# Raw weights behind the branch, units 4 to 7 placed before r*k, middle units gathered in float32

## The chip, the cores and the metric

One core of one Trainium2 chip runs the whole program as one launch. The time is device microseconds of that core, the median over several executions; the kernel before is at 474.01 us (472.36 to 475.83).

## The reference

Three layers follow one another: a linear recurrence with heads (2 batches, 8 heads, 768 steps, 48 wide), a mixture of 8 experts in which each token goes to one, and a gated MLP.

```python
for t in range(S):                      # recurrence, per batch and head
    cur = einsum('bhd,bhe->bhde', u * k_t, v_t)
    y[:, :, t] = einsum('bhd,bhde->bhe', r_t, state + cur)
    state = w_t[..., None] * state + einsum('bhd,bhe->bhde', k_t, v_t)
x = y as (N = 1536 tokens, D = 384)
logits = x @ w_gate; e = argmax(logits); gate = softmax(logits)[e]
# token i takes the next free slot of its expert (at most `capacity`, 384)
h = relu(x[slots of e] @ w1[e]); out = gate * (h @ w2[e])    # F = 1024
g = out @ w_gate2; result = (silu(g) * (out @ w_val)) @ w_out   # d_ff = 1536
```

## The kernel before

The tokens are cut into 12 units of 128 (u = 0 to 11), six per batch. For each unit the recurrence is done in chunk form: `scores` makes the masked matrix A on TensorE, ScalarE and GpSimd, `values` multiplies it with v and adds the carried state (`Sb`, written by `expand`), `own` and `xrow` add the token's own term, `r*k` (`prep3`, line 428) feeds `diag`, which gives that own term's factor. `gate_t` transposes x, `logits` (or `gate_rows` with `columns`) makes the gate's 8 logits.

Units are chosen in groups: 0 to 3, 4 to 7 ("four"), 8 and 9 ("two"), 10 and 11 ("last"). `choose` takes the maximum, the one-hot `ohs` and the softmax's weight on VectorE and ScalarE; `count` makes running counts on TensorE; `place` turns them into slots. `weigh` makes the weighted rows `xg` on ScalarE (line 593), and `scatter` writes them to `scr` in HBM by an indirect DMA from GpSimd (line 751), into the experts' slots.

Expert 0's input does not go through HBM for the last four units: `onehot` (line 806) compares a unit's slots with a row of column numbers, and `x0_add` (line 829) gathers x transposed, straight into PSUM, with the one-hot as the moving side. There x is split into a high and a low fp32r half: `x0_high` on ScalarE (line 815), `x0_low` on GpSimd for units 8 and 9 (line 821) and on VectorE for 10 and 11 (line 823). The units before come back from `scr` into `zrow` (`x0_load`) and are added with the identity, in float32. `parts` splits the result into `xe0`.

Weights are raw float32 tiles of 768 KB, loaded by SyncE's queue (`load_raws`, line 169) into three pools: `RAWS = 5, 2, 3` buffers, one of the first five being xe0's. ScalarE casts a piece to its high half (`high`, line 207) and VectorE subtracts for the low half (`low`, line 212). In the unit loop six are loaded; the last pool lies where the recurrence's tiles lay, so it opens behind `early.close()`. `st["held"]` stops further loads. When both halves of a raw tile are made, `low` calls for more loads.

Program order on each engine is what the text writes, except that short VectorE steps kept in `steps` are put in by `tick` and `flush`. `tc.mark_branch_hint_location` announces the branch `tc.If(most > SLOTS)`, into which the program would go if an expert had more than 240 tokens; all engines read a count and compare (line 1239). Behind it the experts run: `m1` (line 1300), `relu`, `m2` (line 1318), with `fill` and `need` putting in the weights' steps, then the MLP (lines 1413 and 1436). `warm` issues 512-column matmuls whose result is not used (line 452).

The tail of the attention, lines 948 to 1066, is written out by hand and is where nearly all of the change lies. Of the PSUM tiles there, the counts and logits of units 4 to 11 share one tile, `lgs`.

Of the kernel before, what the change touches and what calls it, by code (L numbers as in the profile page):

```python
# [26 lines left out]
NU = N // C  # L27
# [15 lines left out]
def build(tc, cap, dm, tk, vt, ub, cst, wg, w1, w2, wgate, wval, wout, out):  # L43
# [113 lines left out]
    def load_raws(upto):  # L157
        while not st["held"] and st["loaded"] < min(upto, len(raws_)):
            free_ = [p for p in rps if len(p[2]) < p[1] or p[2][-p[1]] in done]
            if not free_:  # L160
                return
            free_[0][2].append(st["loaded"])
            src = raws_[st["loaded"]]
            t = raw_t[st["loaded"]] = free_[0][0].tile([128, 1536], F32, tag="raw", name="raw")
            if len(src.shape) == 3 and src.dtype != F32:
                k = src.shape[1]
                nc.sync.dma_start(out=t.bitcast(I32).rearrange("p (k f) -> p k f", k=k), in_=src.bitcast(I32))
            else:
                nc.sync.dma_start(out=t.rearrange("p (k f) -> p k f", k=src.shape[1]), in_=src)
            st["loaded"] += 1  # L170
# [382 lines left out]
            nc.tensor.matmul(ps[32 * k:32 * k + 32], wgs[:, k, :], xgt[w][:, k, :], start=False, stop=True,  # L553
                             skip_group_check=True)

    lgs = []

    def logits_to(u):
        g = group[u]
        if g not in lgt:  # L560
            if g[-1] < NU - 5:
                lgt[g] = ps1.tile([128, len(g), 3 * E], F32, tag="lg", name="lg")
            else:
                i = g[0] % 4 + 4 * (g[0] > 7)
                if not i:
                    lgs.append(ps1.tile([128, 8, 3 * E], F32, tag="lg", name="lg"))
                lgt[g] = lgs[0][:, i:i + len(g)]
        return lgt[g][:, u - g[0]]

    def logits(u):  # L570
# [69 lines left out]
    def chosen_of(us):  # L640

        n = len(steps)
        w = []
        choose(us, lambda us, sm: w.extend([*weigh(us, sm), sm]) or w)
        new = steps[n:]
        del steps[n:]
        return new[:5], [new[5], *w[:2]], w[2:-1], w[-1]
# [169 lines left out]
    def x0_low(q, w):  # L817

        hi, lo = xhl[q]
        if q in xgs:  # L820
            nc.gpsimd.tensor_tensor(out=lo, in0=xgs[q], in1=R(hi), op=ALU.subtract)
            return
        nc.vector.scalar_tensor_tensor(out=lo, in0=xt[q], scalar=w, in1=R(hi), op0=ALU.mult, op1=ALU.subtract)

    def x0_add(x, rhs, c0, first=False, last=False, ks=range(3)):
# [62 lines left out]
    for u in range(NU - 2):  # L888
        chosen, counted = ended.get(u - 2), ended.get(u - 3)
        if u:  # L890
            prep0(u + 2)
            prep1(u + 2)
        xrow(u - 1)
        state(u)
        anchored(u + 2)
        warm((7, 4)[u] if u < 2 else 3, ps1, "xT")
        scores(u + 1)
        if u:
            own(u)
        kgtok(u + 1)  # L900
        if u:
            gate_t(u - 1, (u - 2 if u > 1 else None, u + 1))
        else:
            psr = ps1.tile([128, 2 * C], F32, tag="xT", name="psr")
            gs = gp.tile([128, DM + C], F32, tag="xT", name="gs", bufs=3)
            for q in range(2):
                diag(q, psr[:, C * q:C * q + C], True)
            nc.scalar.copy(out=gs[:, 0:2 * C], in_=psr)
            gss.update((q, gs[:, C * q:C * q + C]) for q in range(2))
            warm(2, ps1, "lg")  # L910
        expand(u)
        load_dm(u + 4)
        zero(NZ)
        if counted:
            count(counted)
            place(counted)
            ready += counted
        prep2(u + 2)
        if not u:
            check(1)  # L920
            nc.vector.tensor_copy(out=tri, in_=before)
        check(u + 2)
        if u:
            values(u)
            columns(u - 1, max(u - 2, 0), u + 1)
        else:
            values(u)
            for q in range(2):
                to = logits_to(q)
                nc.tensor.matmul(to[:, 0:E], gss.pop(q), fold[:, E:2 * E], start=True, stop=True)  # L930
            a8 = gp.tile([128, 2, H], F32, tag="a82", name="a82")
            nc.scalar.copy(out=a8, in_=lgt[group[0]][:, 0:2, 0:E])
            for q in range(2):
                a8s[q] = a8[:, q, :]
            own(0)
        if chosen:
            flush()
            if u < NU - 3:
                choose(chosen)
        load_v(u + 3)  # L940
        if u >= 4:
            load_raws(2 * (u - 4) + 1)
        if u >= 5:
            fill(0.0)
        for _ in range(2):
            if ready and not steps:
                scatter(ready.pop(0))
# [6 lines left out]
        nc.gpsimd.memset(col[:, cap:], -1.0)  # L954
    four, two, last = (ended[q] for q in (7, 9, 11))
    c4, sums4, rows4, _ = chosen_of(four)
    own(u, nc.vector)
    xrow(u - 1)
    state(u)
    prep3(u + 1)  # L960
    early.close()
    more_raws(RAWS[2])
    load_raws(len(raws_))
    st["held"] = True
    values(u, [0])
    warm(1, ps1, "xT")
    scores(u + 1)
    for f in c4:
        f()
    gate_t(u - 1)  # L970
    psr = ps1.tile([128, C], F32, tag="xT", name="psr")
    gate_rows(u - 2, u + 1, psr)
    gss[u - 1] = gp.tile([128, C], F32, tag="gs", name="gs", bufs=1)
    nc.scalar.copy(out=gss[u - 1], in_=psr)
    expand(u)
    values(u, [1, 2, 3])
    columns(u - 1, u - 2, u + 1)
    count(four)
    for f in sums4:
        f()  # L980
    place(four)
    flush()
    for f in rows4[:2]:
        f()
    values(u + 1, [0, 1, 2])
    xrow(u)
    own(u + 1, nc.vector)
    for q in (*ready, *four[:2]):
        scatter(q)
    gate_t(u)  # L990
    values(u + 1, [3])
    xrow(u + 1)
    logits(u - 1)
    for f in rows4[2:]:
        f()
    for q in four[2:]:
        scatter(q)
    x0_load()
    gate_t(u + 1)
    c2, sums2, rows2, sm2 = chosen_of(two)  # L1000
    for f in c2:
        f()
    logits(u)
# [2 lines left out]
    for f in (*bases, *sums2, *placed):  # L1006
        f()
    judge()
    for i, q in enumerate(two):
        x0_high(q, sm2[:, i, :])  # L1010
    tc.mark_branch_hint_location("rare", engines=[PE, SP])
    logits(u + 1)
    warm(3, ps1, "T")
    c, sums, rows, sm = chosen_of(last)
    for f in c:
        f()
    for i in range(2):
        onehot(i, *(x[:, i, :] for x in at2))
    for f in rows2:
        f()  # L1020
    for i, q in enumerate(two):
        x0_low(q, sm2[:, i, :])
    for f in later:
        f()
    for q in two:
# [5 lines left out]
    tc.mark_branch_hint_location("rare", engines=[DVE, ACT, POOL])  # L1031
    for i, q in enumerate(last):
        x0_high(q, sm[:, i, :])
    warm(1, ps1, "T")
    for i, q in enumerate(two):
        x0_add(xhl[q][0], hot[0][:, i, :], 0, first=not i)
    flush()
    totals(ps1, ones, (ohacc, *(ohs[:, q, :] for q in (*two, *last))), odds, "P")
    warm(2, ps1, "T")
    for i in range(2):  # L1040
        onehot(2 + i, *(x[:, i, :] for x in atl))
    for i, q in enumerate(last):
        x0_add(xhl[q][0], hot[0][:, 2 + i, :], 0)
    for i, q in enumerate(last):
        x0_low(q, sm[:, i, :])
    for i, q in enumerate(two):
        x0_add(xhl[q][1], hot[0][:, i, :], 0)
    x0_add(xhl[last[0]][1], hot[0][:, 2, :], 0)
    offsets(one8)
    for i in range(2):  # L1050
# [285 lines left out]

    xet[0] = xe0
    x_load(1)
    st["held"] = False
    load_raws(len(raws_))  # L1340
    for e in range(E):
        if e == 4:
            end_raws()
        for f in range(8):
            if f % 4 == 0:
                need(("w1", e, f // 4))
            m1(e, f)
            if f % 4 == 3:
                free(("w1", e, f // 4))
            if f:  # L1350
                relu(e, f - 1)
            elif e:
                for d in range(3):
                    put_y(ypt.pop((e - 1, d)), d, reg, 0, SLOTS)
                reg = off_reg(e)
            if e and f in (2, 5):
                x_trans(e + 1, int(f > 2))
            fill(0.5)
        if not e:
            done.add("xe0")  # L1360
            reg = off_reg(e)
        relu(e, 7)
        x_load(e + 2)
        if e < E - 1:
            for f in range(8):
                if f % 4 == 0:
                    need(("w2", e, f // 4))
                m2(e, f)
                if e == 0 and f in (1, 3):
                    x_trans(1, int(f == 3))  # L1370
                if f % 4 == 3:
                    free(("w2", e, f // 4))
                if (e, f) == (3, 4):
                    nc.scalar.activation(out=lut, in_=ident[:, 0:1], func=AF.Silu)
                fill(0.9 if e else 0.7)
        else:
            for j in range(2):
                need(("w2", e, j))
            for d in range(3):
                for f in range(8):  # L1380
                    m2(e, f, [d])
                    if d == 2 and f % 4 == 3:
                        free(("w2", e, f // 4))
                put_y(ypt.pop((e, d)), d, reg, 0, SLOTS)
                part(0, d)
                fill(2.0)
# [169 lines left out]
```

## Time and profile before

| | |
|---|---|
| median of 3 runs | 474.01 us (472.36 to 475.83) |
| the profiled execution, its own time | 476.68 us |
| its span, first to last instruction | 475.0 us |
| mean granted TensorE clock | 0.983 |
| TensorE busy | 454.4 us (96%) |
| VectorE busy | 332.5 us (70%) |
| ScalarE busy | 240.4 us (51%) |
| GpSimd busy | 72.8 us (15%) |
| DMA | 62.57 MB, 132 GB/s over the span |

The profile is of one execution. A busy engine says little about what sets the end: this needs the chain of waits and the timeline of each stretch. The clock is the share of 2.4 GHz that the chip granted TensorE. The start of an instruction is recorded, the end of a matmul is modelled. A releaser is inferred from semaphore events.

### The profile page before, as it was taken

The page shows a single profiled execution, that of the slowest core. Times are in us where ns is not written, and L with a number is a line of the kernel's source. Part 1 is how long each engine was busy: PE and PEld are TensorE (multiplying, and loading weights), DVE is VectorE, ACT ScalarE, POOL GpSimd, SP SyncE. Part 2 cuts the span into 40 slices and gives each one's busy share as a digit, 9 for nine tenths or more (in the row PEclk, how much of TensorE's full clock was granted, in tenths as well). Part 3 has the DMA queues.
Part 4 walks back from the last instruction along what each step waited for, and adds up shares of the span by engine and source line. Part 5 has one row for each costly group of instructions (what it writes and reads, how often), then busy time and mean ns, then how long its engine had stood idle before and what let it go on. Part 6 is the DMA issues. An engine that isn't in the chain of part 4 may idle for free.

```text
span 475.0 us, 9312 instructions
## 1 busy us (share of the span) xinstructions
PE 454.4 (96%) x3583; PEld 400.7 (84%) x3594; DVE 332.5 (70%) x690; ACT 240.4 (51%) x563; POOL 72.8 (15%) x96
## 2 busy tenths in 40 slices
PE   7998898789999999999999999999999999999994
PEld 3677676668999999999988888888888888888884
DVE  8999998475798759559779966575868576434241
ACT  4566774435788677665455465353625333221220
POOL 3423464370000000000000370000000000003033
PEclk9999999869999999999999999999999999999999
DMA  7899994727888966107333424042200000001011
GB/s 242 230 272 276 318 252 146 268 87 225 270 283 268 344 245 195 70 1 227 106 84 117 71 64 128 8 127 72 66 1 1 2 0 1 0 1 67 0 68 66
DMA packets 33649, 62.57 MB, mean 132 GB/s; under 512 B 5216, under 2 KB 16992, under 8 KB 33600
## 3 DMA queue, kind: packets, MB, share of 16 engines
q1 hardware_dynamic: 31680, 57.20, 39.5%
q0 software_dynamic: 1920, 4.73, 2.7%
q8 instruction: 29, 0.48, 0.5%
q14 instruction: 20, 0.16, 0.1%
HBM read 52.48 MB, written 9.44 MB: 130 GB/s over the span
## 4 chain that ended last, share of the span: by engine, by line
PE 72%; issue 2%; DVE 1%; POOL 1%; POOLq 0%; ACT 0%
PE psg L1413 31%; PE psu L1436 14%; PE pso L1318 14%; PE psh L1300 13%; POOL out L1448 1%; PE psx L1285 1%; DVE wu L212 1%; DVE acc L1446 0%; POOLq L1552 0%; DVE h L1307 0%; ACT h L1306 0%; POOLq L1448 0%
## 5 line engine op out<-in xcount | busy, mean ns | idle before, releaser
L1413 PE MATMUL psg<-yb,wu 128*128 128x512 f32 x648 | 156.3, 395 | 0.0
L1413 PEld LDWEIGHTS psg<-yb,wu 128*128 128x128 f32 x648 | 121.3, 188 | 26.2
L1436 PE MATMUL psu<-wu,a 128*128 128x384 f32 x432 | 80.8, 336 | 0.0
L1436 PEld LDWEIGHTS psu<-wu,a 128*128 128x128 f32 x432 | 76.4, 188 | 2.9
L1300 PE MATMUL psh<-xe,wu 128*128 128x240 f32 x576 | 69.7, 277 | 2.0 <-ACTq L1239 1.4
L1300 PEld LDWEIGHTS psh<-xe,wu 128*128 128x128 f32 x576 | 66.3, 190 | 2.7 <-ACTq L1239 1.5
L1318 PE MATMUL pso<-h,wu 128*128 128x240 f32 x576 | 66.7, 275 | 0.3 <-DVE wu L212 0.3
L1318 PEld LDWEIGHTS pso<-h,wu 128*128 128x128 f32 x576 | 65.4, 189 | 0.5 <-DVE wu L212 0.5
L1420 DVE TENSOR_TENSOR t<-t,psg 128x512 f32<-128x512 f32 x36 | 24.7, 686 | 52.6 <-PE psg L1413 34.9
L212 DVE TENSOR_TENSOR wu<-raw,wu 128x512 fp32r<-128x512 f32 x96 | 61.4, 684 | 0.0
L207 ACT CAST wu<-raw 128x512 fp32r<-128x512 f32 x96 | 54.8, 621 | 5.3 <-DMA raw<-in_moe_w 1.5
L1425 ACT CAST a<-t 128x512 fp32r<-128x512 f32 x36 | 22.3, 619 | 58.7 <-DVE t L1420 55.7
L1307 DVE SCALAR_TENSOR_TENSOR h<-psh,h 128x240 fp32r<-128x240 f32 x64 | 24.9, 402 | 24.7 <-ACT h L1306 24.4
L1333 POOL DMA_INDIRECT idl<-ids,dests x12 | 13.4, 1120 | 165.5 <-DVE bits L187 162.2
L1448 POOL DMA_INDIRECT out<-acc,idc x12 | 11.7, 976 | 174.1 <-DVE acc L1446 172.3
L207 ACT CAST wu<-bits 128x384 fp32r<-128x384 f32 x36 | 18.0, 514 | 40.0 <-DVE bits L200 38.7
L1419 ACT ACTIVATE t<-psg 128x512 f32<-128x512 f32 x36 | 21.5, 596 | 26.9 <-PE psg L1413 26.9
L1426 DVE TENSOR_TENSOR a<-t,a 128x512 fp32r<-128x512 f32 x36 | 24.8, 689 | 11.7 <-ACT a L1425 11.0
L1306 ACT ACTIVATE h<-psh 128x240 fp32r<-128x240 f32 x64 | 23.2, 373 | 10.5 <-PE psh L1300 9.7
L1446 DVE TENSOR_TENSOR acc<-psu,acc 128x384 f32<-128x384 f32 x24 | 12.9, 558 | 20.9 <-PE psu L1436 20.9
L452 PE MATMUL psW<-xinit,ones 128*128 128x512 bf16 x49 | 18.5, 466 | 4.0 <-DVE ones L862 3.0
L465 ACT COPY A<-psA 128x512 f32<-128x512 f32 x24 | 12.8, 587 | 18.3 <-PE psA L463 18.3
(155 smaller groups left out, 563.6 us busy)
## 6 DMA issues: line engine op xcount, KB each, us to landing
raw<-in_moe_w SPq DMA_DIRECT2D x32, 768.0 KB, 6.0
dm<-in_dm SPq DMA_DIRECT2D x18, 291.0 KB, 6.8
scr<-zrow SPq DMA_DIRECT2D x12, 384.0 KB, 6.5
raw<-in_moe_w_gate SPq DMA_DIRECT2D x6, 768.0 KB, 4.6
raw<-in_moe_w_val SPq DMA_DIRECT2D x6, 768.0 KB, 6.4
raw<-in_moe_w_out SPq DMA_DIRECT2D x6, 768.0 KB, 4.3
v<-in_tk SPq DMA_DIRECT2D x12, 192.0 KB, 7.3
dm<-in_dm SPq DMA_DIRECT2D x3, 512.0 KB, 3.7
```

What stands on the lines that cost most here:

```text
L207: nc.scalar.copy(out=slot_t[u % NSLOT][:, 0, c:c + n], in_=bits[i])
L212: nc.vector.tensor_tensor(out=w[:, 1, c:c + n], in0=bits.pop(i), in1=R(w[:, 0, c:c + n]), op=ALU.subtract)
L1300: nc.tensor.matmul(ps, w[:, a, k, c0:c0 + 128], xet[e][:, b, k, :], start=n == 0, stop=n == 8)
L1306: nc.scalar.activation(out=h[:, 0, :], in_=ps, func=AF.Relu)
L1307: nc.vector.scalar_tensor_tensor(out=h[:, 1, :], in0=ps, scalar=0.0, in1=R(h[:, 0, :]), op0=ALU.max, op1=ALU.subtract)
L1318: nc.tensor.matmul(ypt[e, d], w[:, a, f % 4, 128 * d:128 * d + 128], h[:, b, :], start=f == 0 and n == 0, stop=f == 7 and n == 2)
L1413: nc.tensor.matmul(gps[i][g], w[:, a, g, k, c0:c0 + 128], yb[t, k][:, c], start=a_ == k == 0, stop=a_ == k == 2)
L1419: nc.scalar.activation(out=t, in_=pg[0], func=AF.Silu)
L1420: nc.vector.tensor_tensor(out=t, in0=t, in1=pg[1], op=ALU.mult)
L1425: nc.scalar.copy(out=a[:, 0], in_=t)
L1426: nc.vector.tensor_tensor(out=a[:, 1], in0=t, in1=R(a[:, 0]), op=ALU.subtract)
L1436: nc.tensor.matmul(out_ps[t, j], att[i][:, c, 128 * j:128 * j + 128], w[:, a, f % 4, :], start=f % FP == 0 and n == 0, stop=f % FP == FP - ...
```

## The change

- `logits_to`: each group has a PSUM tile of its own; that of units 8 and 9 takes the tag of the state's tile ("P"), also that of `totals`.
- `x0_low` has no GpSimd branch any more; units 8 and 9 have no high and low halves, they are gathered from `xgs` with the one-hot read as float32. Their weighted rows are made ahead of the hint.
- The load in the unit loop is capped at raw tile 6; the pool of three opens behind the branch, and the first m1 issues one load at f = 0, 3 and 6.
- r*k of unit 11 stands behind the choice of units 4 to 7; their counts, sums and places stand ahead of the gate rows' columns; the scatters of two of them ahead of the last values.
- Of the warm-ups, two come ahead of `gate_t(u + 1)` and two ahead of `logits(u + 1)`; one and two behind the second hint go. The first hint (for TensorE and SyncE) stands behind `logits(u + 1)`.

```diff
     def logits_to(u):
         g = group[u]
         if g not in lgt:
-            if g[-1] < NU - 5:
-                lgt[g] = ps1.tile([128, len(g), 3 * E], F32, tag="lg", name="lg")
-            else:
-                i = g[0] % 4 + 4 * (g[0] > 7)
-                if not i:
-                    lgs.append(ps1.tile([128, 8, 3 * E], F32, tag="lg", name="lg"))
-                lgt[g] = lgs[0][:, i:i + len(g)]
+            lgt[g] = ps1.tile([128, len(g), 3 * E], F32, tag="P" if g[-1] == NU - 3 else "lg", name="lg")
@@ x0_low
-        if q in xgs:
-            nc.gpsimd.tensor_tensor(out=lo, in0=xgs[q], in1=R(hi), op=ALU.subtract)
-            return
@@ unit loop
-            load_raws(2 * (u - 4) + 1)
+            load_raws(min(2 * (u - 4) + 1, RAWS[0] + RAWS[1] - 1))
@@ tail
+    st["held"] = True
     own(u, nc.vector)
     xrow(u - 1)
     state(u)
-    prep3(u + 1)
-    early.close()
-    more_raws(RAWS[2])
-    load_raws(len(raws_))
-    st["held"] = True
     values(u, [0])
     warm(1, ps1, "xT")
     scores(u + 1)
     for f in c4:
         f()
+    prep3(u + 1)
+    early.close()
     gate_t(u - 1)
+    values(u, [1, 2, 3])
+    count(four)
     psr = ps1.tile([128, C], F32, tag="xT", name="psr")
     gate_rows(u - 2, u + 1, psr)
...
     expand(u)
-    values(u, [1, 2, 3])
-    columns(u - 1, u - 2, u + 1)
-    count(four)
     for f in sums4:
         f()
     place(four)
     flush()
+    columns(u - 1, u - 2, u + 1)
     for f in rows4[:2]:
         f()
-    values(u + 1, [0, 1, 2])
+    for q in (*ready, *four[:2]):
+        scatter(q)
+    values(u + 1, [0, 1])
     xrow(u)
     own(u + 1, nc.vector)
-    for q in (*ready, *four[:2]):
-        scatter(q)
     gate_t(u)
-    values(u + 1, [3])
+    values(u + 1, [2, 3])
     xrow(u + 1)
     logits(u - 1)
+    warm(2, ps1, "xT")
...
     judge()
-    for i, q in enumerate(two):
-        x0_high(q, sm2[:, i, :])
+    for f in rows2:
+        f()
+    warm(2, ps1, "T")
+    logits(u + 1)
     tc.mark_branch_hint_location("rare", engines=[PE, SP])
-    logits(u + 1)
     warm(3, ps1, "T")
...
-    for f in rows2:
-        f()
-    for i, q in enumerate(two):
-        x0_low(q, sm2[:, i, :])
     for f in later:
         f()
...
-    warm(1, ps1, "T")
     for i, q in enumerate(two):
-        x0_add(xhl[q][0], hot[0][:, i, :], 0, first=not i)
+        x0_add(xgs[q], R(hot[0][:, i, :]), 0, first=not i)
+    for i in range(2):
+        onehot(2 + i, *(x[:, i, :] for x in atl))
     flush()
     totals(ps1, ones, (ohacc, *(ohs[:, q, :] for q in (*two, *last))), odds, "P")
-    warm(2, ps1, "T")
-    for i in range(2):
-        onehot(2 + i, *(x[:, i, :] for x in atl))
...
-    for i, q in enumerate(two):
-        x0_add(xhl[q][1], hot[0][:, i, :], 0)
@@ behind the branch
-    st["held"] = False
-    load_raws(len(raws_))
+    more_raws(RAWS[2])
     for e in range(E):
...
             if f % 4 == 0:
                 need(("w1", e, f // 4))
+            if not e and f in (0, 3, 6):
+                st["held"] = False
+                load_raws(st["loaded"] + 1)
+                st["held"] = f < 6
             m1(e, f)
```

## Rows read from the trace of the kernel before

**Rows 1.** The page's first line.

```profile
span 475.0 us, 9312 instructions
```

**Rows 2.** The chain that ended last, in order of time: start, us, what.

```profile
106.69 3.30 PE psh L1300 x27
```

**Rows 3.** Stretches: busy us (instructions) of each engine, granted clock, DMA share, GB/s.

```profile
86.00:90.00 4.00, 3.24 (x51) 2.71 (x46) 2.82 (x12) 1.58 (x5) 2.19 (x2) 1.00 1.06 388
90.00:94.00 4.00, 1.94 (x17) 1.88 (x17) 1.26 (x8) 1.90 (x6) 1.96 (x3) 0.55 0.62 234
...
99.00:104.00 5.00, 5.00 (x23) 4.37 (x21) 3.59 (x11) 1.38 (x4) 3.64 (x7) 0.50 0.22 80
104.00:107.00 3.00, 1.63 (x14) 1.45 (x13) 1.82 (x4) 1.28 (x4) 1.91 (x2) 0.99 0.30 108
```

**Rows 4.** Timeline, 81 to 88 us: start, us, engine, line, operation, [idle before <-releaser].

```profile
81.54 0.68 DVE L428 TENSOR_TENSOR rk<-dm 128x512 f32<-128x512 f32 x1
...
82.35 1.22 POOL L466 TENSOR_SCALAR_AFFINE_SELECT A<-A 128x512 f32<-128x512 f32 x2 [3.92 <-ACT A L465]
...
85.40 0.39 PE L488 MATMUL y<-Sb,M 128*64 128x96 f32 x4
...
85.58 0.19 DVE L670 TENSOR_SCALAR t<-lg 128x32 f32<-128x32 f32 x1 [1.45 <-ACT xg L593]
...
87.51 0.52 PE L541 MATMUL psx<-ident,x 128*128 128x128 f32 x3 [0.71 <-DVE x L527]
```

**Rows 5.** Timeline, 90 to 94 us.

```profile
90.29 0.16 DVE L703 TENSOR_SCALAR end<-be 128x2 f32<-128x2 f32 x1
...
90.70 0.17 PE L657 MATMUL lg<-ohacc,ones 128*128 128x8 bf16 x1
...
92.61 0.18 DVE L710 TENSOR_TENSOR t<-lg,ohs 128x16 f32<-128x16 f32 x1 [1.43 <-remote]
...
92.93 1.42 PE L573 MATMUL lg<-wgs,xT 128*128 128x8 f32 x6 [2.06 <-ACT xhl L815]
```

**Rows 6.** Timeline, 95 to 100 us.

```profile
95.31 1.49 DVE L806 TENSOR_SCALAR hot<-col,end,sl 128x240 fp32r<-128x240 f32 x2
95.67 2.00 POOL L821 TENSOR_TENSOR xhl<-xg,xhl 128x384 fp32r<-128x384 f32 x2 [3.10 <-PE psW L452]
...
96.72 0.97 DVE L703 TENSOR_SCALAR end<-be 128x2 f32<-128x2 f32 x1
...
98.19 1.12 ACT L815 ACTIVATE xhl<-x,sm 128x384 fp32r<-128x384 f32 x2 [2.05 <-DVE sm L588]
...
99.11 0.71 DVE L806 TENSOR_SCALAR hot<-col,end,sl 128x240 fp32r<-128x240 f32 x2
```

**Rows 7.** Timeline, 99 to 107 us.

```profile
99.66 3.74 PE L829 MATMUL x<-hot,xhl 128*128 128x240 f32 x16
...
103.20 1.01 PE L829 MATMUL x<-ident,zrow 128*128 128x128 f32 x4
...
104.17 0.60 PE L829 MATMUL x<-ident,zrow 128*128 128x128 f32 x4
...
105.36 0.36 ACT L834 CAST xe<-x 128x240 fp32r<-128x240 f32 x1 [0.20 <-PE x L829]
...
106.69 4.63 PE L1300 MATMUL psh<-xe,wu 128*128 128x240 f32 x39 [1.37 <-ACTq L1239]
```

**Rows 8.** Timeline near 19 us: r*k beside GpSimd.

```profile
18.90 1.31 DVE L428 TENSOR_TENSOR rk<-dm 128x512 f32<-128x512 f32 x1
...
18.68 0.99 POOL L443 TENSOR_TENSOR aV<-v,a 128x384 f32<-128x384 f32 x1 [2.01 <-ACT a L932]
```

**Rows 9.** Raw loads: the page's issues (KB each, median us to landing), then two timelines.

```profile
raw<-in_moe_w SPq DMA_DIRECT2D x32, 768.0 KB, 6.0
...
82.31 1.48 SPq L169 DMA_DIRECT2D raw<-in_moe_w  x3
...
121.99 3.22 ACT L207 CAST wu<-raw 128x512 fp32r<-128x512 f32 x6
```

More of the change, by code (lines that the diff above doesn't have):

```diff
@@ L554, in gate_rows @@
                              skip_group_check=True)
-    lgs = []
     def logits_to(u):
@@ L999, in build @@
     gate_t(u + 1)
-    c2, sums2, rows2, sm2 = chosen_of(two)
+    c2, sums2, rows2, _ = chosen_of(two)
     for f in c2:
```

## The prediction

> **What bounds the kernel now.** I read the chain of waits first. From 106.69 us on it is almost nothing but TensorE: the first expert's m1 starts there, and the work behind it is the same after the change [rows 2]. So the question is only what the edits do to the moment at which that first m1 starts. Next I read the stretches: until 90 us TensorE has the full clock; then the granted clock falls to its lower level (0.55 as a mean over 90 to 94 us, which puts the fall near 90.4) and stays at 0.50 until about 104 [rows 3]. The timelines say what holds the way to 106.69:
>
> - Units 4 to 7 are placed late: VectorE idles 1.45 us until 85.58, and TensorE waits 0.71 us for x of unit 10 before its gate transposes at 87.51 [rows 4].
> - The counts of units 8 and 9 are recorded on TensorE at 90.70, but VectorE gets them only at 92.61, and TensorE does not start the logits of unit 11 before 92.93. Of this 2 us hole no row names a plausible cause: the releaser given for TensorE, line 815, has nothing to do with its operands [rows 5]. The hint on the branch stands just there.
> - From the end of the last logits (92.93 + 1.42 = 94.35, called T) to the weighted rows of the last units VectorE works one long queue. Its two one-hots take 1.49 us and the tiny line 703 takes 0.97 us while GpSimd makes the low halves (95.67 to 97.67); the same pair of one-hots takes 0.71 us at 99.11 [rows 6].
> - From 99.66 to about 105.3 TensorE is the limit: 16 gather matmuls in 3.74 us, then the rest; the last copy out of PSUM ends at 105.72, and after the branch m1 starts at 106.69 [rows 7]. T to the end of the gather is 11.0 us.
>
> **Parts of the change, priced.**
>
> *Raw weights.* Three loads leave 82.31 us [rows 9] and are issued one at a time in the first m1 instead. I cost this at nothing. The first cast that reads the seventh raw tile is the fifth of six in the row at 121.99, so near 124.1. Issued by about 109 and landed 6.0 us later (the median), it has 9 us to spare; the later two are read later still, each behind at most one wait for a buffer. If that cover went, the cast would block ScalarE's queue and with it the relu copies that free PSUM. Removing the loads gives nothing back directly either: what they ran beside (the scatters on GpSimd) is not what the gather waits for. On SyncE's queue they now stand behind the first read of expert 1's rows and ahead of the second expert's; a load that waits for a buffer holds that read, which is not needed until two m1 steps into expert 1. The scatters that come earlier have nothing ahead of them on GpSimd's queue, and nobody waits for them before the zrow part of the gather. The cap in the unit loop changes nothing, as there are only six buffers then.
>
> *Placing units 4 to 7 ahead of r\*k.* VectorE's choosing starts at 81.6 instead of 82.14 (behind r\*k), the counts come before columns, and the idle 1.45 us shrinks: slots about 1 us earlier. But the gate rows now stand behind the counts, so the copy of them and expand stand later on ScalarE, and values of unit 11, which needs expand, start near 85.9 instead of 85.40. Behind it wait the gate transposes of unit 10; their own 0.71 us wait is gone, since x is early. I get these transposes at 86.8 instead of 87.51, the two warm-ups (0.45 us) and the transposes of unit 11 at 89.2 instead of 89.34, and the counts of 8 and 9 at 90.75 instead of 90.87: gain 0.1 us; bounds 0 and the 0.7 us that the transposes gain.
>
> r\*k itself goes from 81.54 under GpSimd's two selects at 82.35 [rows 4]. Under a two-input GpSimd operation the same instruction took 1.31 us instead of 0.68 [rows 8]. The Trainium skill's page "SBUF — State Buffer", section "SBUF: two separate sides", speaks against the move: VectorE and GpSimd lock a port pair for a whole instruction. By that rule r\*k would end up to 0.63 us later; TensorE is busy with values and counts until about 84.1 then, so by row or rule the sum moves by 0.2 us at most.
>
> *Two warm-ups ahead of the last logits.* They stand on the path. At half clock the six logits matmuls took 1.42 us [rows 5]; a 512-column warm-up should take, by its columns against a 240-column gather matmul (0.23 us at half clock, below), 0.45 us at half clock and 0.23 at full. Cost 0.45 us at full clock, 0.9 at half.
>
> The three warm-ups that go from behind the hints ran while TensorE waited for ScalarE's high parts; I cost them at nothing.
>
> *The 2 us hole.* Not shown by cause, so bounded: it stays (it follows the hint or the code around it, and stands behind the last logits then) or goes. I keep it with about 7 in 10, because the hint and the code remain. Half clock: counts 90.75, warm-ups to 91.65, logits to 93.05, hole 1.7: T is 94.75 against 94.35, a loss of 0.4. Without the hole T is 93.05, a gain of 1.3.
>
> *No low halves on GpSimd.* The one-hots fall by 1.49 - 0.71 = 0.78 us and line 703 to the 0.16 that it took at 90.29 [rows 5]: 0.8. So the sums of the last units, and ScalarE's high parts (98.19), come 1.6 us sooner after T. The two high parts of units 8 and 9 on ScalarE are replaced by the two plain weighted rows which were made later: no change there.
>
> *Gather in float32.* Removed: 12 matmuls (6 high, 6 low) at 3.74 / 16 = 0.23 us at half clock. Added: 6 float32 matmuls, two instructions each, of 240 columns. The trace shows float32 of 128 and 112 columns: four in 1.01 us at half clock and in 0.60 at full [rows 7], 0.25 and 0.15 each with the tail of the last in it. Scaled by 240/120 that is at most 0.50 and 0.30 for an instruction; the one-pass gather matmul of 240 columns (0.23, half of it at full) is the least. I take 0.40 and 0.21, near the upper end, as the tail is about a quarter of the quoted rows. So 4.8 us at half clock, 2.5 at full (bounds 2.8 to 6.0 and 1.4 to 3.6), against 2.8 and 1.4 removed. The skill's page "FP8 and Floating Point Precision", section "TensorE Precision Notes", gives true FP32 four passes: by that my estimate would be 6 x 4 x 0.23 = 5.5 us at half clock. But these matmuls can start when the one-hots exist, at T + 1.8 (the one-hots now start at 95.31, T + 1.0, and take 0.7), and run while VectorE and ScalarE prepare the last units, where TensorE had idled. Half clock: T + 1.8 + 4.8, totals 0.2, so T + 6.8. Before, TensorE worked without a break from 99.66 and the clock rose near 104; here the unbroken work starts at T + 1.8, so I take the rise at about T + 6.5. What is left (12 gather matmuls, 12 float32 ones of zrow) costs 12 x 0.12 + 12 x 0.13 = 3 us at full clock: end at T + 9.9 against T + 11.0, gain 1.1. Full clock throughout: T + 1.8 + 2.5 + 0.2 + 3 = T + 7.5, gain 3.4.
>
> **Sum of the likeliest.** Clock falls again: -0.4 + 1.1 = 0.7 us gained with the hole, 1.3 + 1.1 = 2.4 without; weighted to the first, 1.3. The profiled execution took 476.68 us (span 475.0 [rows 1]), 0.6% over the median of 474.01; the gain lies inside the span, and I take it off the median: 472.7 us, its own range 471 to 474.5.
>
> **Rivals.**
>
> 1. *The clock stays up.* For it: four more warm-ups lie in the stretch (86 to 94) in which it fell. Against: TensorE was busy for 3.24 of 4.00 us from 86 to 90 and the clock fell right behind that, and the hole may stay. With the hole T is 90.75 + 0.45 + 0.8 + 1.7 = 93.7 (the logits at about 0.8 as their columns are few), gain 0.65 + 3.4 = 4.0, 470.0 us; without the hole 5.7, 468.3 us.
> 2. *Nothing moves.* m1 starts when ScalarE is through the branch, 1 us behind its last copy, and when VectorE has made the last weights' low half; VectorE's queue there is as long as before. If it decides, the gather's gain is lost: 474.
> 3. *Slower: float32 at half clock, and the clock not back.* If the clock stays low through the gather, it ends at T + 6.8 + 12 x 0.23 + 12 x 0.23 = T + 12.3, a loss of 1.3; with T's 0.4 and the first 27 m1 matmuls (3.30 us at full clock) at half, from 1.7 up to 5.0 us: 475.7 to 479. It decides if the clock comes back later than about T + 9. Against it: the gather is now unbroken from T + 1.8.
>
> **Numbers.** Forecast 0.55; clock stays up 0.28; nothing moves 0.10; slower 0.07. The range reaches from 468.3 (rival 1 without the hole) to 476 (the third rival's gather and T alone). One per cent is 4.7 us, about what a measurement of this kernel can tell from no change. Faster by more: rival 1 in its stronger half and a little of the forecast, 0.19. Slower by more: rival 3 in its upper half and what I overlooked, 0.08. Within 1%: 0.73.
>
> **What would show it.** Right, if the granted clock is 0.5 somewhere from 90 to 100 us, the one-hots after the last logits take 0.71 us a pair, line 703 some 0.16, 12 float32 gather instructions take 0.4 us each, and the first m1 starts near 105.4. A hole behind the last logits says that it follows the hint; none says that the raw loads or their place made it. Wrong, if ScalarE or TensorE waits for a raw tile between 106 and 135, if r\*k delays the gate rows past 85, if the clock stays at 1.0 from 80 to 105 (then rival 1), or if m1 starts at half clock (rival 3).

## The result, and the profile after

| | kernel before | changed kernel |
|---|---|---|
| median of 20 runs, us | 473.95 (472.00 to 477.93) | 470.36 (from 468.91) |
| ratio, 95% interval | | 0.9919 [0.9897, 0.9942] |
| profiled execution, us | 476.68 | 469.3 |
| its mean granted clock | 0.983 | 0.997 |
| scores(11) start, us | 80.50 | 79.44 |
| last logits read by VectorE, us | 94.39 | 90.58 |
| first m1, us | 106.69 | 99.33 |

In the medians the changed kernel takes 0.8% less time. Which chip this was is not known. Sixteen of its 20 runs lie from 468.9 to 472.3 at a granted clock of 0.994 or more, three from 474.6 to 476.3 at 0.983 to 0.984, and one at 1137.78 us is disturbed.

The page's first line and the stretches answer [rows 1] and [rows 3]; the columns are the same.

```profile
span 467.6 us, 9307 instructions
...
86.00:90.00 4.00, 3.95 (x53) 3.43 (x52) 1.95 (x11) 2.39 (x8) 3.09 (x4) 1.00 0.28 102
90.00:94.00 4.00, 3.52 (x27) 2.83 (x28) 3.40 (x20) 2.48 (x7) 1.63 (x5) 1.00 0.41 130
99.00:104.00 5.00, 4.63 (x39) 4.44 (x39) 2.37 (x7) 3.60 (x9) 3.10 (x6) 1.00 0.28 105
```

TensorE is busy for 3.95 and 3.52 of 4 us where it was for 3.24 and 1.94, and the clock never leaves its upper level between 8 and 465 us. The timeline from 81 to 91 us answers [rows 4, 5]:

```profile
81.30 1.23 POOL L466 TENSOR_SCALAR_AFFINE_SELECT A<-A 128x512 f32<-128x512 f32 x2 [3.84 <-ACT A L465]
81.90 1.17 DVE L428 TENSOR_TENSOR rk<-dm 128x512 f32<-128x512 f32 x1
83.49 0.16 DVE L662 TENSOR_SCALAR t<-lg 128x32 f32<-128x32 f32 x1
84.81 0.39 PE L488 MATMUL y<-Sb,M 128*64 128x96 f32 x4 [0.21 <-ACT Sb L521]
...
87.21 0.98 POOL L743 DMA_INDIRECT scr<-xg,slots  x1 [0.30 <-issue]
87.33 0.56 DVE L527 TENSOR_TENSOR x<-y,aV 128x384 f32<-128x384 f32 x1 [1.61 <-ACT xg L585]
88.86 0.48 ACT L546 COPY xT<-psx 128x384 f32<-128x384 f32 x1 [1.03 <-PE psx L541]
...
89.82 0.73 PE L565 MATMUL lg<-wgs,xT 128*128 128x8 f32 x6
89.98 0.15 DVE L702 TENSOR_TENSOR t<-lg,ohs 128x16 f32<-128x16 f32 x1
90.58 0.17 DVE L608 TENSOR_REDUCE mx<-lg 128x2 f32<-128x16 f32 x1 [0.25 <-PE lg L565]
```

r\*k takes 1.17 us under GpSimd's selects (0.68 before). The 2.06 us in front of the last logits are gone: they start at 89.82 with no wait, and VectorE's product (L702, before L710) comes at 89.98 without one. From 91 us on, answering [rows 6, 7]:

```profile
91.51 0.71 DVE L798 TENSOR_SCALAR hot<-col,end,sl 128x240 fp32r<-128x240 f32 x2
92.05 2.67 PE L818 MATMUL x<-hot,xg 128*128 128x240 f32 x12
92.14 0.16 DVE L695 TENSOR_SCALAR end<-be 128x2 f32<-128x2 f32 x1
92.81 1.12 ACT L807 ACTIVATE xhl<-x,sm 128x384 fp32r<-128x384 f32 x2 [1.43 <-DVE sm L580]
...
98.22 0.36 ACT L823 CAST xe<-x 128x240 fp32r<-128x240 f32 x1 [0.20 <-PE x L818]
99.33 0.94 PE L1281 MATMUL psh<-xe,wu 128*128 128x240 f32 x6 [1.15 <-ACTq L1220]
...
105.86 2.47 SPq L169 DMA_DIRECT2D raw<-in_moe_w  x3
...
114.62 3.22 ACT L207 CAST wu<-raw 128x512 fp32r<-128x512 f32 x6
```

The one-hots take 0.71 (1.49), the small line 0.16 (0.97), the float32 gather 2.67 us for 12 instructions, and the last two rows, which answer [rows 9], show the late raw loads and casts that wait for none.

**Where 7.4 us of span went.** The points between which this is counted, two rows of before and one of after:

```profile
80.50 1.16 PE L463 MATMUL psA<-M 64*128 64x128 f32 x16
94.39 0.17 DVE L616 TENSOR_REDUCE mx<-lg 128x2 f32<-128x16 f32 x1 [1.40 <-PE lg L573]
...
79.44 1.16 PE L463 MATMUL psA<-M 64*128 64x128 f32 x16
```

scores(11), the products that make unit 11's matrix A, starts 1.06 us sooner (80.50 to 79.44; a load of inputs landed that much sooner, which the change does not touch). From scores(11) to VectorE's reading of the last logits it is 11.14 us in place of 13.89, 2.75 less; from there to m1 8.75 in place of 12.30, 3.55 less. Behind m1 the two are alike to 0.01 us. The experiments divide the second and third number.

### The profile page after: what moved, and what is told of

It reads as the page before. It is cut to its first block, busy times and chain, and to the rows that moved or that the text cites. A ratio compares the mean times of both kernels' runs of the same rounds, so it can differ in the third digit from the quotient of the medians.

```text
span 467.6 us, 9307 instructions
## 1 busy us (share of the span) xinstructions
PE 451.0 (96%) x3584; PEld 398.1 (85%) x3595; DVE 330.8 (71%) x690; ACT 239.4 (51%) x561; POOL 70.2 (15%) x94
## 4 chain that ended last, share of the span: by engine, by line
PE 74%; issue 2%; DVE 1%; POOL 1%; POOLq 0%; ACT 0%
PE psg L1397 31%; PE psu L1420 14%; PE pso L1299 14%; PE psh L1281 13%; POOL out L1432 1%; PE psx L1266 1%; DVE wu L212 1%; DVE acc L1430 0%; POOLq L1536 0%; DVE h L1288 0%; ACT h L1287 0%; POOLq L1432 0%
## 5 line engine op out<-in xcount | busy, mean ns | idle before, releaser
L1311 DVE TENSOR_TENSOR yb<-yT,yb 128x512 fp32r<-128x512 f32 x27 | 18.5, 684 | 4.4 <-ACT yb L1310 4.4
```

## Experiments

Each kernel was run against the kernel before on the same chip: the first four on one chip, then four on a second, four on a third. The kernel named as a control is the changed kernel itself on that chip; the first chip has none. The profiles are one execution each.

**The kernel before, twice.** No edit.

> The kernel before, unchanged, with a second profile. If the 1.7 us between the counts of units 8 and 9 and their use on VectorE, the 1.06 us by which the last dm tile came late at 74.4 us, and the fall of the clock near 90 belong to the kernel, all three are there again and the first m1 starts at 106 to 107 us. If they belong to that one execution, the first m1 starts up to 2.8 us earlier, at 104 or so. The fall of the clock, at least, should be there again: about 474 us.

Measured: 475.47 us against 474.48, ratio 1.0033 [1.0006, 1.0060]: 0.3% lies between two equal kernels. Its profile has no hole: with scores(11) at 82.69, the last logits start 0.64 us after the count is there and VectorE reads them at 94.13, 11.44 us later (13.89 in the profile of before). So the hole does not come with that order of work alone: this execution has the hint, the code and the early raw loads of before, and no hole. The clock falls all the same, from 77.9 to 81.3 us and from 94.9 to 101.8.

```profile
93.29 0.81 PE L573 MATMUL lg<-wgs,xT 128*128 128x8 f32 x6 [0.64 <-DVE t L710]
94.13 0.17 DVE L616 TENSOR_REDUCE mx<-lg 128x2 f32<-128x16 f32 x1 [0.79 <-PE lg L573]
...
94.00:99.00 5.00, 3.48 (x28) 2.38 (x28) 4.34 (x18) 2.56 (x8) 3.22 (x7) 0.59 0.38 131
```

**The changed kernel without its early warm-ups.**

```diff
     logits(u - 1)
-    warm(2, ps1, "xT")
...
-    warm(2, ps1, "T")
     logits(u + 1)
```

> The changed kernel without its two early pairs of warm-ups (behind the logits of unit 9 and ahead of those of unit 11). Theory W, that these matmuls keep the clock up: it falls to 0.5 near 90 us, the 12 float32 gather instructions take about 0.4 us each instead of 0.22, and the time is 474 to 476 us. Rival H, that TensorE simply has fewer gaps by the other edits: the clock stays at 1.0 and the time is 469 to 470.4 us, 0.3 to 0.9 us less by the warm-ups' own time.

Measured: 471.12 us, ratio 0.9925 [0.9896, 0.9955], clock 0.994 in five of seven runs, where the kernel before has 0.987 (median) on this chip. The gain is there without the warm-ups, so it does not rest on them. The profile is of the slowest run (476.25 us): scores(11) starts at 85.12, and the clock is low from 79.9 to 86.7 and from 96.9 to 100.4. So it does not show what the clock did in the runs near the median.

**The kernel before with the two early warm-ups.**

```diff
     logits(u - 1)
+    warm(2, ps1, "xT")
...
+    warm(2, ps1, "T")
     tc.mark_branch_hint_location("rare", engines=[PE, SP])
     logits(u + 1)
```

> The kernel before with the two early pairs of warm-ups added and nothing else. Theory W: the clock stays up; the gather part, 5.6 us at half clock, falls to about 3.2, and the logits and warm-ups behind 90 us gain 1 more, less 0.9 for the warm-ups themselves: about 471 to 472 us. Rival H: the clock falls as before, and the added matmuls cost up to 0.9 us: 474 to 475 us.

Measured: 474.07 us, ratio 0.9998 [0.9968, 1.0029]: warm-ups alone bring nothing. Its profile (472.57 us) has the old order of work at full clock throughout and so gives a price: from reading the last logits (92.55) to m1 (102.58) 10.03 us, against 12.30 in before and 8.75 in after.

```profile
92.55 0.17 DVE L616 TENSOR_REDUCE mx<-lg 128x2 f32<-128x16 f32 x1 [0.72 <-PE lg L573]
102.58 0.60 PE L1302 MATMUL psh<-xe,wu 128*128 128x240 f32 x3 [1.15 <-ACTq L1241]
```

**The changed kernel with three raw loads ahead of the branch again.**

```diff
     early.close()
+    st["held"] = False
+    more_raws(RAWS[2])
+    load_raws(len(raws_))
+    st["held"] = True
...
```

(the loads in the first m1 go)

> The changed kernel with the three raw loads put back ahead of the branch, right behind the end of the early tiles, and the loads in the first m1 as before. Theory, that where the raw tiles are loaded costs nothing: 470.4 us within 0.7. Rival R, that three loads at 82 to 91 us hold up the scatters or the code fetch: a gap of 1 to 2 us on TensorE near 90 us is back, the clock falls, and the time is 472 to 475 us.

Measured: 473.65 us, ratio 0.9957 [0.9912, 1.0001], the clock anywhere from 0.976 to 0.999. In its profile the piece from scores(11) to m1 is 19.80 us, as in after (19.89); what is late is scores(11), 84.18, since the inputs of unit 11 landed at 76.5. That load is issued ahead of the raws in question. So in this execution the raws cost nothing where they were moved. But the median lies in rival R's range and not in that of the theory; it is 2.5 us above the sibling without warm-ups on that chip, with intervals that overlap, and the changed kernel itself was not run there. Whether the place of the raws costs anything in the median stays open.

**The changed kernel again, on two more chips.** No edit.

> The changed kernel itself once more, as the measure for the other three and for the spread. Two theories of the spread. D: the load of dm(11) lands between 73.3 and 76.7 us from one profiled execution to the next (before 74.40, after 73.34, two variants 76.5 and 76.7), which moves scores(11) from 79.4 to 85.1 us, and where the matrix engine has been idle for it the clock falls at 78 to 80 us; nothing of the change touches this. Then the time of scores(11) to m1 is what the change moved: 26.2 us before, 19.9 after. D expects 470.4 +- 0.7 again, a granted clock of 0.994 to 0.999 in most runs, and runs above 473 only where the clock is 0.990 or less. Rival C: the difference between chips or days is as large as the change's effect; then the median comes out at 472 or more, as two variants of the changed kernel (471.1 and 473.7) did on another chip.

> The changed kernel once more, as the control of this chip. On the chip of the record it took 470.4 us against 474.0 before; on the second chip it took 475.5 against 476.1, and its profile there has the release of y(11) by the matrix engine (end 89.45) reach VectorE only at 90.96, 1.51 us late, with a 16 KB refill of the matrix engine's instructions under way from 89.43 to 90.87, and the clock falling at 93.2 behind it. Theory F (a release that meets a refill of code is held about 1.5 us; which release that is hangs on where in the instruction stream the 16 KB end, and the change moved this from the count of units 8 and 9 (1.72 us late before) to y(11)): the hold is there again at y(11) or it is not, and the time follows it: 470 to 471.5 without, 474 to 476 with it. Rival R (the hold has nothing to do with the refill and falls anywhere): it is found at another release.

Measured: 475.51 against 476.08, ratio 0.9995 [0.9966, 1.0023]; and 476.51 against 475.49, ratio 1.0037 [1.0002, 1.0073]. The gain is gone. The timeline of the first of the two, against the rows of after above:

```profile
89.37 0.84 PE L565 MATMUL lg<-wgs,xT 128*128 128x8 f32 x6
89.43 0.97 POOL L743 DMA_INDIRECT scr<-xg,slots  x1 [0.30 <-issue]
90.70 0.97 POOL L743 DMA_INDIRECT scr<-xg,slots  x1 [0.30 <-issue]
91.04 0.56 DVE L527 TENSOR_TENSOR x<-y,aV 128x384 f32<-128x384 f32 x1 [3.11 <-PE lg L565]
91.75 0.52 PE L541 MATMUL psx<-ident,x 128*128 128x128 f32 x3 [1.31 <-DVE x L527]
91.97 0.97 POOL L743 DMA_INDIRECT scr<-xg,slots  x1 [0.30 <-issue]
92.47 0.18 DVE L608 TENSOR_REDUCE mx<-lg 128x2 f32<-128x16 f32 x1 [0.86 <-PE psx L541]
93.98 0.48 ACT L546 COPY xT<-psx 128x384 f32<-128x384 f32 x1 [3.93 <-PE lg L649]
96.64 0.17 DVE L608 TENSOR_REDUCE mx<-lg 128x2 f32<-128x16 f32 x1 [1.18 <-PE lg L565]
```

The products of unit 11 end on TensorE at 89.45, but VectorE's sum (L527) begins at 91.04; the logits of unit 9 end at 90.21 and are read at 92.47; the transposes end at 92.27 and are copied at 93.98. Three results in a row reach their readers 1.6 to 2.3 us late (in the second case VectorE is busy with the late sum until 91.60); in after they take 0.10 us or less. On the third chip it is the same three. From scores(11) to reading the last logits it takes 14.98 us, on the third chip 14.93, in after 11.14. Behind the first of them TensorE runs dry, and the clock falls: at 93.2 us on the second chip, at 91.2 on the third.

```profile
90.00:94.00 4.00, 1.80 (x17) 1.42 (x19) 1.51 (x7) 0.07 (x2) 2.33 (x3) 0.90 0.43 161
94.00:99.00 5.00, 4.49 (x22) 3.15 (x22) 2.87 (x18) 2.31 (x9) 0.75 (x4) 0.50 0.26 77
```

Rival C's number came out (the difference between chips or days is as large as the change's effect); each chip was used in one stretch of time, so chip and day are not told apart.

In the semaphore events of all 14 profiles up to 110 us, about 320 of TensorE's releases (the signals by which it tells the readers of a result that it is there) fall into an indirect DMA that GpSimd is issuing or within 0.4 us of one: 55 of these are recorded over 0.4 us behind the recorded end. Of about 1400 others none is. Five profiles have none, though they have 141 releases at such places, none of them over 0.05 us late: after, b0, e1, e2, e3. The other nine, the profile of before among them, have 4 to 8 each. All four profiles of the first chip are without, all eight of the second and third have them, whichever of the two orders of work they run; only the profiles of before and after, on chips not known, differ. So what some executions have and others not may as well belong to the chip or the day.

The hole of [rows 5] is such a release: the count of units 8 and 9 ends at 90.87, its release is recorded at 92.59, and GpSimd issues scatters from 87.51 to 92.57. Standing beside scatters is not enough for it: in that same profile the three results that come late in the new order are read in time, with scatters under way.

```profile
88.67 0.56 DVE L527 TENSOR_TENSOR x<-y,aV 128x384 f32<-128x384 f32 x1 [0.84 <-PE y L493]
89.36 0.17 DVE L616 TENSOR_REDUCE mx<-lg 128x2 f32<-128x16 f32 x1
89.98 0.48 ACT L546 COPY xT<-psx 128x384 f32<-128x384 f32 x1 [0.42 <-PE psx L541]
```

The Trainium skill's page "Perfetto Trace Analysis", section "Summary: the profiler window per engine type", says that a TensorE row ends at an estimated time and leaves the travel of its semaphore out; the trace agrees, and here what lies between that end and the reading is 0.1 us in one execution and 1.6 in another. As the end is an estimate, the trace does not tell whether the result or only its signal was late.

**The changed kernel with one shared PSUM tile of logits.**

```diff
-            lgt[g] = ps1.tile([128, len(g), 3 * E], F32, tag="P" if g[-1] == NU - 3 else "lg", name="lg")
...
+                lgt[g] = lgs[0][:, i:i + len(g)]
```

> The changed kernel with the logits of units 8 to 11 in one shared PSUM tile again, so that logits(11) has to wait for VectorE's product of two (L710), as in the kernel before, where that came 2.06 us late. Theory H (the hole of 2 us ahead of logits(11) is this dependency, together with the late release of the product): logits(11) waits about 2 us again, m1 starts 22 us behind scores(11) in place of 19.9, the clock may fall behind it, 472.4 or more. Rival T (the tile alone puts only the product's own time ahead of logits(11), the late release belonged to the old order): logits(11) 0.3 to 0.9 us later, 470.4 to 471.3, m1 20.2 to 20.8 us behind scores(11).

Measured: 475.83 us, the same as its control (475.51); scores(11) to m1 24.66 and 24.67 us. Its products of unit 11 are read 1.61 us late, the control's 1.59. In the new order the shared tile costs nothing that shows: theory T's side, with the hole elsewhere. The times of both theories were missed.

**The kernel before with tiles of their own for the logits**, the reverse edit.

> The kernel before with nothing changed but the PSUM tiles of the logits: units 8 and 9, unit 10 and unit 11 each have their own, so logits(11) has no reason to wait for VectorE's product of two (L710). Theory H (the 2.06 us ahead of logits(11) came through this dependency, with the count of two released 1.72 us late): logits(11) follows the count at once, last logits near 92.3 in place of 94.35 if scores(11) is at 80.5, scores(11) to m1 at most 24 us in place of 26.2, and 1 to 2.5 us less than the kernel before: ratio 0.995 to 0.998. Rival N (the logits of 11 wait for something else just as long, or the one-hots and GpSimd behind them take up the gain): ratio 0.999 to 1.001.

Measured: 474.09 against 475.49, ratio 0.9971 [0.9951, 0.9991]; scores(11) to m1 23.65 us. The ratio lies in theory H's range, but it is no further from 1 than that of two equal kernels on the first chip (1.0033). So theory H rests on the rows:

```profile
89.74 0.83 PE L565 MATMUL lg<-wgs,xT 128*128 128x8 f32 x6
...
91.05 0.17 DVE L702 TENSOR_TENSOR t<-lg,ohs 128x16 f32<-128x16 f32 x1 [0.68 <-PE lg L565]
...
92.56 0.17 DVE L608 TENSOR_REDUCE mx<-lg 128x2 f32<-128x16 f32 x1 [1.13 <-PE psW L452]
```

The last logits now run right behind the count, at 89.74, although VectorE's product is still late. So the shared tile was the way by which one late release reached TensorE: theory H, for the path in the kernel, not for why a release is late. But the logits end at 90.57 and are read at 92.56: their own release is late now, so that from scores(11) to that reading only 1.6 us are gained (12.33 against 13.89).

**The changed kernel with units 8 and 9 gathered by halves again.**

```diff
+    for i, q in enumerate(two):
+        x0_high(q, sm2[:, i, :])
...
-        x0_add(xgs[q], R(hot[0][:, i, :]), 0, first=not i)
+        x0_add(xhl[q][0], hot[0][:, i, :], 0, first=not i)
...
+        x0_add(xhl[q][1], hot[0][:, i, :], 0)
```

(the low halves are taken on GpSimd, behind the one-hots in the program)

> The changed kernel with units 8 and 9 gathered by high and low halves again, the low ones taken by GpSimd beside the one-hots, everything else as changed. Theory L (VectorE is what the path goes through behind the last logits, and GpSimd's low halves slow it: one-hots 1.49 in place of 0.71 us, L703 0.97 in place of 0.16): last logits to m1 1.6 us longer, 10.4 in place of 8.8, less what the matrix engine saves where it waits (12 float32 instructions of 0.22 us against 12 of 0.11); 471.2 to 472.0. Rival P (the matrix engine is what the path goes through there at full clock): the halves save it up to 1.3 us, 469.1 to 470.4.

Measured: 477.09 against 475.51 of its control, 1.6 us more, ratio to before 1.0023 [0.9994, 1.0051]. The size is theory L's. The one profile is of an execution of 481.17 us, 4.1 above that median; in it the place is another, as GpSimd runs ahead and meets the choosing of the last units.

```profile
99.33 1.95 POOL L813 TENSOR_TENSOR xhl<-xg,xhl 128x384 fp32r<-128x384 f32 x2 [3.97 <-ACT xg L585]
99.45 0.90 DVE L615 SCALAR_TENSOR_TENSOR eq<-ls,csb 128x16 f32<-128x16 f32 x1
100.39 0.17 DVE L621 TENSOR_REDUCE be<-eq 128x2 f32<-128x16 f32 x1
100.59 0.71 DVE L624 TENSOR_TENSOR ohs<-eq,be 128x16 bf16<-128x16 f32 x1
101.23 0.71 DVE L798 TENSOR_SCALAR hot<-col,end,sl 128x240 fp32r<-128x240 f32 x2
```

L615 and L624 take 0.90 and 0.71 us (0.17 each beside no GpSimd work), 1.3 us more on the path; the reduction between them, which has one input, takes its 0.17. The Trainium skill's page "SBUF — State Buffer", section "SBUF: two separate sides", states that an instruction of VectorE with two inputs in SBUF and one of GpSimd that reads SBUF lock each other out of a port pair for a whole instruction: the trace agrees, both slow ones have two inputs.

**The changed kernel with two raws behind the inputs of unit 11.**

```diff
-            load_raws(min(2 * (u - 4) + 1, RAWS[0] + RAWS[1] - 1))
+            load_raws((1, 2, 3, 5, 6, 6)[u - 4])
```

> The changed kernel with two of the five raw weights that stand ahead of dm(11) in SyncE's queue put behind it (one raw is 768 KB, about 2 us of all transfer engines at 390 GB/s, which are full from 40 to 75 us). Theory D (dm(11) lands late because the raws are ahead of it): it lands 2 to 4 us sooner, no wait of ScalarE and VectorE for it at 71 to 73 us, scores(11) near 78.4 and not past 79.5 in any profile, no clock fall at 78 us, 468.5 to 469.5 with a spread under 2 us. Rival Q (its landing is set by how many transfers share the engines, not by their order, or the decoding of raws then waits and delays the units): scores(11) as before or later, 470.4 to 473.

Measured: 475.47 us, as its control. The wait for the inputs at 72 to 75 us is gone and scores(11) starts at 79.81 (81.66 in the control's profile), but the sum of unit 11 is 1.59 us late here too, the clock falls at 89.9, and scores(11) to m1 is 25.61 us against 24.67. Theory D explains when scores(11) starts, not the time.

**Code shifted: 90 more TensorE instructions ahead of unit 10**, alone and together with the later raws.

```diff
-            nc.tensor.matmul(ps, ones, x, start=True, stop=True)
+            for j in range(0, 512, 128 if fine else 512):
+                j = slice(j, j + (128 if fine else 512))
+                nc.tensor.matmul(ps[:, j], ones, x[:, j], start=True, stop=True)
```

> The changed kernel with the warm-up instructions of units 2 to 6 cut in four (twelve of 128 columns in place of three of 512, the same columns), which puts 90 more instructions of the matrix engine ahead of unit 10, so the refill of code that fell on the end of y(11) falls some 90 instructions earlier, into the first half of the products of y(11), where no release is due for over 1 us. Theory F: no release of y(11) late by 1.5 us; on a chip where the control shows the hold and takes 474 to 476, this takes 470.5 to 473; where the control shows none, the same as the control within 0.5. Rival R (the hold is not tied to the refill): y(11) held as in the control, or another release at random, and no difference to the control. The cut warm-ups themselves may cost up to 0.2 us a unit where the matrix engine is what the unit waits for, 1 us in all.

> e8 together with the later raw weights of e7 (two of the five raws that stood ahead of dm(11) put behind it), as the candidate for the better kernel. e7 alone showed scores(11) at 79.8 us with no wait for dm(11), but the hold at y(11) and two falls of the clock behind it, 475.5. Theory D and F together: scores(11) at 78.5 to 80, no hold at y(11), no fall of the clock near 78 or 90 us: 469 to 471 with a spread under 3 us, less than the control by 3 to 5 us where that shows the hold, by 0 to 1.5 where it does not. Rival R: as the control.

Measured: 480.58 and 480.69 us, ratios 1.0109 [1.0085, 1.0133] and 1.0119 [1.0084, 1.0154]. Theory F falls: in the control the products of unit 11 end at 88.17, the 16 KB refill of TensorE's instructions runs from 88.28 to 89.32, and the release is 1.5 us late, as the theory has it. But in the second of these two the refill runs from 86.47 to 87.42, over 0.39 us before the products of unit 11 end (87.81), and these are read 1.61 us late all the same; in the first it ends at 89.35, the products end at 89.68, and they are read 0.6 us late. In after a refill is under way from 87.38 to 88.32, and the release of 88.00 in it is in time. Most of the slowdown is at the branch. TensorE's rows of m1 in the first of the two:

```profile
108.67 2.04 PE L1283 MATMUL psh<-xe,wu 128*128 128x240 f32 x8 [3.40 <-PEq L1222]
111.38 4.83 PE L1283 MATMUL psh<-xe,wu 128*128 128x240 f32 x28 [0.68 <-issue]
```

TensorE's own sequencer (PEq) is what m1 waits for, 3.4 us (the control's row names ScalarE's, 1.3), and behind eight matmuls it stops for 0.7 us with nothing to wait for; the clock falls at 107.8. Refills are recorded from 105.46 to 106.71 and from 108.93 to 110.16, where the control has only the first, so the end of a 16 KB piece now seems to lie just behind the branch; that is argued from these times, not shown. From m1 to the MLP it takes 138.9 and 139.3 us in these two, 135.6 to 135.8 in the others.

## Why the prediction was right and where it was not

The time (470.4) and the sign are in the range and within 1%, but the likeliest case (472.7, its own range 471 to 474.5) was not what the record's profile shows. It shows rival 1: the clock stays up and the hole is gone, for which the prediction had 468.3 us, a gain of 5.7; between the medians it is 3.6, between the two profiled executions 7.4. That the median lies near the forecast is in part luck: the change's own work comes to 1.6 us by the sum below, and the rest depends on late releases and a clock that differ from profile to profile.

- **The hole.** This is the step that failed: kept with 7 in 10, "because the hint and the code remain". In b0 the hint and the code are the same and there is no hole; in after the hint stands behind the last logits and leaves none. The hole is a late release of TensorE, passed on by the shared tile (e6). That such releases come late only beside GpSimd's scatters, and only in some profiles, was in no row that I had read. The sign "none says that the raw loads or their place made it" fails too: b0 and e3 have the loads ahead of the branch and no hole.
- **The clock.** That it would fall again near 90 us did not happen in after, e2 and e3. It happened on the second and third chip, at 93.2 and 91.2 in the unchanged pair, and m1 started at 106.3 and 106.5 (the forecast said 105.4). Late releases alone do not explain it: in before it falls at 90.4, ahead of the hole, and in b0 and e1, where no release is late, it falls at 94.9 and 96.9. What made it stay up in after is open; the gain does not need the warm-ups, for which rival 1 was argued (e1), and they bring none by themselves (e2).
- **Low halves off GpSimd.** Right to 0.02 us: 1.49 to 0.71, 0.97 to 0.16; the halves put back cost 1.6 us in all (e5).
- **Float32 gather.** 0.22 us an instruction at full clock (2.67 / 12) against 0.21 forecast; 0.41 at half clock on the third chip (4.95 / 12) against 0.40. From the end of the last logits to the start of the last copy out of PSUM 7.67 us (98.22 - 90.55), forecast T + 7.5.

```profile
96.78 4.95 PE L818 MATMUL x<-hot,xg 128*128 128x240 f32 x12
```

- **Order of units 4 to 7.** Forecast 0.1 us. From scores(11) to reading the last logits, after takes 0.30 us less than the old order without late releases (11.14 and 11.44), with the warm-ups in it. With late releases the new order is the slower, 14.93 to 14.98 against 13.89: the sum of unit 11, the logits of unit 9 and the transposes of unit 11 all come late, where in the profile of before only the count does in this stretch. That loss of 1.1 us was in no rival.
- **r\*k, raw weights.** r\*k 1.17 us and off the path; no cast waits for a raw; both as forecast.
- **Warm-ups.** Priced at 0.45 us at full clock. In the old order scores(11) to reading the last logits takes 0.55 us more with them (11.99 in e2, 11.44 in b0). In the new order the profiles give no price: to the end of the last logits 10.91 us without them (e1, in part at half clock), 11.11 and 10.69 with them (after, e3).
- **Slips in the sums.** 0.7 and 2.4, weighted 7 to 3, give 1.2 and not 1.3; 11.0 - 7.5 is 3.5 and not 3.4; a warm-up by its columns is 0.49 us at half clock and not 0.45. Nothing hangs on these.

**The sum once more.** Of 7.4 us between the two profiles, by the rows above, the late release is 2.45 (13.89 - 11.44; 0.61 of it is the last logits at half clock, 1.42 against 0.81), the clock 2.27 behind the last logits (12.30 - 10.03), the inputs of unit 11 are 1.06, and the change's own work is 0.30 + 1.28 (10.03 - 8.75), 1.6 us. This rests on single profiles. Where releases are late in both kernels, the 1.6 us meet the loss of 1.1 and a clock that is low in both: 0.9995 and 1.0037.

What makes a release late, and why one execution or chip has it and another not, stays open. The test that is left, the scatters of units 4 to 7 moved behind the last logits, was not tried. No kernel here was shown to be faster than before on every chip.

## What to carry to other kernels

Where the trace shows an engine starting well after its operand's recorded end, and names a releaser that has nothing to do with it, look at what else runs at that moment, and look at a second and third profile of the same kernel before giving the gap a price. A result that many wait for is suspect where it is released beside a run of GpSimd's indirect DMAs (moving it away was not tried), and a tile shared by two groups can pass one late reader on to the other (e6). A gain of under 1% in a stretch like this has to be measured on several chips.

## What the hardware showed that was not expected

- TensorE's releases are read 1.6 to 2.3 us late in some executions, only beside indirect DMAs that GpSimd issues (55 of about 320 over 0.4 us late, against none of about 1400); on each of the three chips of the experiments the four profiles agree on whether it happens.
- Ninety more TensorE instructions ahead of a branch, with the same columns, went with 3.3 and 3.7 us more behind it, with a fall of the clock in it (e8, e9); the end of a piece of code there is argued, not shown.
- The same load, issued at 60 us, is waited for until 73.3 us in one profile and 76.7 in another; with 1.5 MB moved out of its way the wait was gone (e7).
